# Splitting a third of the second MLP's weights during the first MLP, with the float64 clamp on GpSimd and buffer pools of its own for each MLP

## The chip, the cores and the metric

One core of one Trainium2 chip runs the whole program. The metric is the device time of one execution in microseconds (us), as the median of several executions. Engines are called by the profile's names: PE is TensorE (matmul), PEld its weight load, DVE VectorE, ACT ScalarE, POOL GpSimd, SP SyncE, which here only issues DMAs.

## What is computed

The reference chains three parts (float64 in, float32 out), cut here to what matters:

```python
# attention with 32 learned memory slots; 4 batches, 8 heads, 576 positions, head size 64
a = softmax(phi, axis=positions);  k_m = a.T @ k;  v_m = a.T @ v
x = softmax(q @ k_m.T / 8) @ v_m            # -> 2304 tokens x 512
h = x @ w_in;  x = (h * sigmoid(1.702 * h)) @ w_out          # MLP A: 512 -> 2048 -> 512
xn = x / sqrt(mean(x * x) + 1e-6) * rms_g
g = xn @ w_gate;  val = xn @ w_val
out = (g * sigmoid(g) * val) @ w_out2                        # MLP B: 512 -> 1536 -> 512
```

## The kernel before, in words

Matmuls run in float32r, three products for one (high x high, low x high, high x low), so every operand exists as a high part `h` (a cast) and a low part `l` (`sub_lo`: the full value minus `h`).

The weights arrive as float64 bit patterns. One half of 128 x 512 values is loaded as a `raw` tile by SP (`w_load`, L137 to L149) and turned into float32 by `to_f32`: the absolute value of the upper word on ACT (L162), then on DVE a clamp (L163), a shift (L167) and two ops that put sign and lower bits together (L171, L174). `w_conv` (MLP A) casts to `h` (`copy`, L113 on POOL or L117 on ACT), subtracts for `l` on POOL (L120) and stores both to a cache in DRAM. `b_split` does the same for MLP B.

The 2304 tokens are worked in two passes (`pr` 0 and 1) of two batches each. MLP A goes through 8 groups of 256 hidden columns in each pass, each group in 4 steps of 288 tokens: `vm_part` folds the attention's values into the weights (L499), `a_g1` makes the hidden values (L531, then `gf` and `gr` by ACT, L537 and L539, and POOL, L120), `a_g2` multiplies by `w_out` (L560) and adds to `x2` on DVE (L568). In pass 0 a group's four weight halves are converted one group ahead, in pass 1 they come back from the cache (`w_again`, L199). The attention of the first two batches runs ahead of MLP A, that of the other two beside its pass 0.

MLP B takes 12 chunks of 128 hidden columns in each pass, with a Strassen-like scheme of seven products: weight tiles 0 to 3 are the gate half, two tiles of sums of gate and value halves (`b_sums`, L231, four DVE ops of 128 x 256) and half a value tile, tile 4 is `w_out2`. One chunk is prepared by `b_prep`: three loads, three `to_f32`, the sums, five `b_split`, each with a store to the cache. `b_unit` makes one chunk for one half of the pass's tokens: seven products on PE (L681), their evacuation on ACT and DVE (L693 to L707), `ph` (L711) and `pl` (L120 on POOL in pass 0, on DVE in pass 1). `b_out` multiplies two chunks by `w_out2` (L733) and adds on DVE (L742). In pass 0 chunk c+1 is prepared beside the units of chunk c; chunk 0 is prepared beside the last group of MLP A. In pass 1 all chunks come back from the cache (`b_again`, L252).

Between the MLPs stand `norm_1` to `norm_4` (squares on ACT, sums on POOL, L585 and L587, scaling on DVE, L627) and `x_sums` and `x_split` (sums and split of the normalised tokens, L647, L658, L120). For pass 0 they run beside MLP A's pass 1, for pass 1 beside MLP B's pass 0, two steps after each unit from chunk 2 on, and `x_sums`/`x_split` of pass 1 with the last chunk.

Each engine and each DMA queue runs its instructions in one fixed order. That order is made at build time by the tile framework's scheduler, from the order in which the program states its steps (the list of steps, `run`, and the loop at the end) and from when a tile of a pool is free. The pools: `raw` 2 tiles, `cv` 5 (work tiles of a conversion), `w` 10 (weight tiles of both MLPs, and work tiles), `gp` 5 (`gr` in MLP A, `ph` in MLP B), `tmp` 4 (`gf` in MLP A, `sg` and `pf` in MLP B).

## Time and profile before

| what | value |
|---|---|
| time, median of 3 runs (lowest to highest) | 948.96 us (948.2 to 949.48) |
| the profiled execution: time, span | 947.55 us, 945.8 us |
| granted TensorE clock, mean | 0.971 of full speed |
| busy share of the span: PE, PEld | 91%, 84% |
| busy share of the span: DVE, ACT, POOL | 71%, 50%, 38% |
| HBM read, written | 97.26 MB, 49.81 MB |

How to read it: the profiled execution lies 1.41 us under the median and 1.75 us over its own span. A busy PE is not a PE at its peak, as matmuls are pipelined, so the shares say less of PE than the distance in time between equal pieces of work. DVE, ACT and POOL stand still for a good part of the span as a whole; what a change is worth depends on the stage it touches. Stretches of time are given as 75:250, in us from the span's start.

### The profile page before, as it was taken

To read this page: it belongs to the slowest core of one execution; us is meant where nothing else is said; L and a number is where in the kernel's file an instruction comes from. 1 tells how busy PE (TensorE), PEld (TensorE's weight loads), DVE (VectorE), ACT (ScalarE), POOL (GpSimd) and SP (SyncE) were. 2 spreads that over 40 slices of the span, in tenths; PEclk is the share of its full clock that TensorE was granted. 3 is DMA by queue.
4 is the path that set the end of the run, shared out by engine and by line. 5 is a ranking of instruction groups with operands and counts; after the bars stand their busy time and mean duration, and the time that the engine had idled before them with its cause. 6 is when DMAs were issued, how large, how long until landed. Compare 5 with 4: busy or idle time off the path is not lost.

```text
span 945.8 us, 16130 instructions
## 1 busy us (share of the span) xinstructions
...
## 2 busy tenths in 40 slices
...
GB/s 213 250 221 90 178 169 230 206 202 210 140 156 90 90 90 89 126 144 114 125 164 189 192 176 171 164 167 134 245 245 89 212 135 122 145 146 132 146 57 100
DMA packets 63966, 148.11 MB, mean 157 GB/s; under 512 B 5776, under 2 KB 30352, under 8 KB 63888
## 3 DMA queue, kind: packets, MB, share of 16 engines
...
HBM read 97.26 MB, written 49.81 MB: 155 GB/s over the span
## 4 chain that ended last, share of the span: by engine, by line
PE 55%; DVE 22%; DMA 8%; ACT 7%; issue 5%; POOL 1%; SPq 1%; ACTq 0%; DVEq 0%; POOLq 0%
PE pg L560 14%; PE pg L733 11%; PE px L681 10%; PE pg L531 8%; PE pw L681 5%; DMA raw_a_in<-in_moe_w_in_dram 4%; PE py L681 3%; DVE cv L171 2%; DVE t L647 2%; DVE cv L174 2%; DVE x L120 2%; DVE s L231 2%; DVE x L568 2%; PE pvm L499 2%; DVE cv L163 2%
## 5 line engine op out<-in xcount | busy, mean ns | idle before, releaser
L560 PE MATMUL pg<-gr,a_outh 128*128 128x288 f32 x1024 | 239.4, 304 | 14.5 <-DVE x L568 9.8
L560 PEld LDWEIGHTS pg<-gr,a_outh 128*128 128x128 f32 x1024 | 177.2, 192 | 20.2 <-DVE x L568 14.2
L681 PE MATMUL px<-x,b_w 128*128 128x256 f32 (+1 forms) x1152 | 182.2, 298 | 12.2 <-ACT sg L693 3.0
L681 PEld LDWEIGHTS px<-x,b_w 128*128 128x128 f32 x1152 | 165.4, 190 | 21.7 <-DVE sg L703 4.2
L120 POOL TENSOR_TENSOR gr<-gf,gr 128x288 fp32r<-128x288 f32 x128 | 111.4, 885 | 128.9 <-ACT gr L539 125.6
L560 PE MATMUL pg<-gr,a_outl 128*128 128x288 f32 x512 | 153.1, 299 | 0.0
L568 DVE TENSOR_TENSOR x<-x,pg 128x288 f32<-128x288 f32 x224 | 98.5, 447 | 52.9 <-PE pg L560 52.1
L733 PE MATMUL pg<-b_w,ph 128*128 128x512 f32 x432 | 132.6, 398 | 2.9 <-DVE oacc L742 2.5
L681 PE MATMUL pw<-x,b_w 128*128 128x320 f32 (+1 forms) x576 | 97.8, 297 | 5.1 <-ACT pf L695 2.7
L560 PEld LDWEIGHTS pg<-gr,a_outl 128*128 128x128 f32 x512 | 98.4, 192 | 0.0
L681 PEld LDWEIGHTS pw<-x,b_w 128*128 128x128 f32 x576 | 84.7, 189 | 8.7 <-ACT pf L695 3.5
L733 PEld LDWEIGHTS pg<-b_w,ph 128*128 128x128 f32 x432 | 78.1, 190 | 16.2 <-DVE oacc L742 3.8
L733 PE MATMUL pg<-b_w,pl 128*128 128x512 f32 x216 | 80.7, 395 | 0.0
L742 DVE TENSOR_TENSOR oacc<-oacc,pg 128x512 f32<-128x512 f32 x90 | 59.4, 680 | 24.5 <-PE pg L733 24.5
L537 ACT ACTIVATE gf<-pg 128x288 f32<-128x288 f32 x128 | 51.7, 411 | 38.6 <-POOL gr L120 18.1
L120 POOL TENSOR_TENSOR b_w<-cv,b_w 128x512 fp32r<-128x512 f32 (+1 forms) x36 | 45.0, 1252 | 62.3 <-ACT b_w L117 56.1
L539 ACT CAST gr<-gf 128x288 fp32r<-128x288 f32 x128 | 52.3, 432 | 28.7 <-PE pg L560 26.7
L163 DVE TENSOR_SCALAR cv<-cv 128x512 f32<-128x512 f32 x68 | 41.4, 613 | 32.2 <-ACT cv L162 32.1
L681 PE MATMUL py<-x,b_w 128*128 128x256 f32 (+1 forms) x288 | 49.4, 300 | 7.0 <-DVE pf L707 5.2
L697 ACT COPY sg<-px 128x256 f32<-128x256 f32 (+1 forms) x48 | 19.1, 398 | 70.9 <-PE px L681 67.8
L711 ACT CAST ph<-pf 128x512 fp32r<-128x512 f32 (+1 forms) x48 | 32.2, 671 | 41.9 <-DVE pf L707 41.7
L681 PEld LDWEIGHTS py<-x,b_w 128*128 128x128 f32 x288 | 42.0, 190 | 10.7 <-DVE pf L707 8.0
...
## 6 DMA issues: line engine op xcount, KB each, us to landing
...
```

The lines of the kernel that those rows point to most:

```text
L120: eng.tensor_tensor(out=lo, in0=full, in1=hi.bitcast(F32), op=ALU.subtract)
L163: nc.vector.tensor_scalar(out=t.bitcast(F32), in0=t.bitcast(F32), scalar1=MINW, scalar2=MAXW, op0=ALU.max, op1=ALU.min,)
L531: nc.tensor.matmul(ps[:, :HALF], lhsT=a[:, b, c, f], rhs=at[:, y, c, n], start=(i == 0), stop=(i == 5),)
L537: nc.scalar.activation(out=gf[:, :HALF], in_=ps[:, :HALF], func=AF.Gelu_apprx_sigmoid)
L539: nc.scalar.copy(out=gr[:, 0], in_=gf[:, :HALF])
L560: nc.tensor.matmul(ps[:, :HALF], lhsT=wo[a][:, fc, es], rhs=gr[fc][:, y], start=(i == 0), stop=(i == 5),)
L568: nc.vector.tensor_tensor(out=acc[:, e, n], in0=acc[:, e, n], in1=ps[:, :HALF], op=ALU.add)
L681: nc.tensor.matmul(ps, lhsT=w[j][:, o : o + P], rhs=xk[k][:, y, xb], start=(first and i == 0), stop=(i == 5), skip_group_check=not (first ...
L697: nc.scalar.copy(out=sg[:, 1], in_=px)
L711: nc.scalar.copy(out=ph, in_=flat)
L733: nc.tensor.matmul(ps, lhsT=lhs, rhs=w[fc][:, y * 512 : y * 512 + 512], start=(i == 0), stop=(i == 5),)
L742: nc.vector.tensor_tensor(out=o, in0=o, in1=ps, op=ALU.add)
```

## The change

- `to_f32` gets an engine for the clamp, POOL by default. In MLP A's pass 0 all clamps but one (`w2[0]`, still DVE) go to POOL; so do those of `gate` and `val` of all MLP B chunks, and that of `o2` for chunks 0 to 3.
- Chunks 0 to 3 of MLP B (`NPRE = 4`) are prepared beside MLP A's pass 1 (`second_side`, three steps after each unit, interleaved with norm and split of pass 0). Their four sums go to POOL too. Their split tiles are only stored to the cache; MLP B's pass 0 reads them back with `b_again`, and prepares chunks 4 to 11 as before.
- The norm of pass 1 runs five steps after each unit from chunk 0 on.
- Pools: MLP A has `rawa` with 3 tiles, `gf` with 3 and `gr` with 5 of the size needed; they are released together with the attention's pools after MLP A, and MLP B's `rawb` 2, `tmp` 4, and `gp` with 5 `ph` and 5 `pl` are laid into that memory. `norm_1` of pass 1 takes its two squares from `tmp` instead of `w`.

```diff
+    NPRE = 4
-    rawp = ctx.enter_context(tc.tile_pool(name="raw", bufs=2))
-    gpp = ctx.enter_context(tc.tile_pool(name="gp", bufs=5))
-    tmp = ctx.enter_context(tc.tile_pool(name="tmp", bufs=4))
+    rawa = tc.alloc_tile_pool(name="rawa", bufs=3, side="right")
+    gfp = tc.alloc_tile_pool(name="gf", bufs=3, side="right")
+    grp = tc.alloc_tile_pool(name="gr", bufs=5, side="right")
...
-    def to_f32(hf):
+    def to_f32(hf, clamp=G):
...
-        nc.vector.tensor_scalar(
+        clamp.tensor_scalar(
             out=t.bitcast(F32), in0=t.bitcast(F32), scalar1=MINW, scalar2=MAXW,
...
-        y = wt.setdefault(("b", c), {})[j] = wtile(f"b_w{j}_{c}")[:, : 2 * n]
+        y = wtile(f"b_w{j}_{c}")[:, : 2 * n]
+        if c >= NPRE:
+            wt.setdefault(("b", c), {})[j] = y
...
-        b_split(c, 4, to_f32(("b", c, "o2")), A, G)
+        b_split(c, 4, to_f32(("b", c, "o2"), G if c < NPRE else V), A, G)
...
-            nc.vector.tensor_tensor(out=out, in0=a, in1=b, op=op)
+            (G if c < NPRE else V).tensor_tensor(out=out, in0=a, in1=b, op=op)
...
-        sq = [wtile(f"sq{i}_{pr}_{t}", F32)[:, : 2 * N] for i in range(2)]
+        sq = [
+            (wtile(f"sq{i}_{pr}_{t}", F32) if pr == 0 else tmp.tile([P, TW], F32, tag="val", name="sq"))
+            [:, : 2 * N] for i in range(2)
+        ]
...
+    def second_side():
+        loads = iter([("b", c, w) for c in range(NPRE) for w in ("gate", "val", "o2")])
+        others = iter([
+            norm_side(0, 0), x_side(0, 0, 0), [*x_side(0, 0, 1), *norm_side(0, 1)],
+            x_side(0, 1, 0),
+        ])
+        for _ in range(2):
+            yield w_load, next(loads)
+        for c in range(NPRE):
+            for s in b_steps(c):
+                yield s
+                hf = next(loads, None) if s[0] in (b_gate, b_val, b_o2) else None
+                if hf:
+                    yield w_load, hf
+            yield from next(others)
...
             if key == ("a", 1, 0) and t == 1:
-                side, per = first_norm(), 2
-            if key == ("a", 1, 7):
-                side, per = prep, 3
+                side, per = second_side(), 3
+            if key == ("a", 1, 7) and t == 1:
+                b_again(0)
...
+    for pool in (grp, gfp, rawa, kmp, vlp):
+        pool.release()
+    two = dict(side="right", reuse_waits="tile")
+    raws[0] = rawb = tc.alloc_tile_pool(name="rawb", bufs=2, **two)
+    tmp = tc.alloc_tile_pool(name="tmp", bufs=4, **two)
+    gpp = tc.alloc_tile_pool(name="gp", bufs=5, **two)
...
-            else:
-                prep = b_prep(c + 1) if pr == 0 else iter([(b_again, c + 1)])
+            elif pr or c + 1 < NPRE:
+                prep = iter([(b_again, c + 1)])
+            else:
+                prep = b_prep(c + 1)
...
-                for s in islice(norms, 2 if c >= 2 else 0):
+                for s in islice(norms, 5):
```

The code moves by up to 23 lines: L163 becomes L165, L113 L115, L120 L122, L231 L235, L252 L258, L199 L201.

**Place 1: POOL in MLP A's pass 0, around the weights of group 6.** `a_6_in` and `a_6_out` are the group's weight tiles, `cv` the work tile of a conversion. Before:

```order
L113 TENSOR_SCALAR a_6_inh<-cv 128x512
L120 TENSOR_TENSOR a_6_inl<-cv,a_6_inh 128x512
L120 TENSOR_TENSOR gr<-gf,gr 128x288 x2
L113 TENSOR_SCALAR a_6_inh<-cv 128x512
L120 TENSOR_TENSOR a_6_inl<-cv,a_6_inh 128x512
L113 TENSOR_SCALAR a_6_outh<-cv 128x512
L120 TENSOR_TENSOR a_6_outl<-cv,a_6_outh 128x512
L113 TENSOR_SCALAR a_6_outh<-cv 128x512
L120 TENSOR_TENSOR gr<-gf,gr 128x288 x2
L120 TENSOR_TENSOR a_6_outl<-cv,a_6_outh 128x512
```

With the change:

```order
L115 TENSOR_SCALAR a_6_inh<-cv 128x512 x2
L122 TENSOR_TENSOR gr<-gf,gr 128x288
L165 TENSOR_SCALAR cv<-cv 128x512 x2
L122 TENSOR_TENSOR gr<-gf,gr 128x288
L122 TENSOR_TENSOR a_6_inl<-cv,a_6_inh 128x512
L115 TENSOR_SCALAR a_6_outh<-cv 128x512
L122 TENSOR_TENSOR a_6_inl<-cv,a_6_inh 128x512
L122 TENSOR_TENSOR gr<-gf,gr 128x288 x2
L327 TENSOR_TENSOR kmisc_0_2166<-kmisc_0_2166 96x768
L115 TENSOR_SCALAR a_6_outh<-cv 128x512
L122 TENSOR_TENSOR gr<-gf,gr 128x288
L165 TENSOR_SCALAR cv<-cv 128x512 x2
```

The clamps (L165) now stand between the splits of `gr` that PE waits for and the splits of the weights; they come in pairs, ahead of the group's own casts.

**Place 2: POOL in MLP A's pass 1, after the norm of the second token tile.** `x_0_0` are split tokens for MLP B, `b_w_1` and `s` its chunk 1. Before:

```order
L120 TENSOR_TENSOR gr<-gf,gr 128x288 x4
L120 TENSOR_TENSOR x_0_0_4145<-x_0_821,x_0_0_4145 128x256
L120 TENSOR_TENSOR gr<-gf,gr 128x288 x2
L120 TENSOR_TENSOR x_0_0_4362<-x_0_821,x_0_0_4362 128x256
L120 TENSOR_TENSOR x_0_0_4145<-t_4140,x_0_0_4145 128x2x256
L120 TENSOR_TENSOR x_0_0_4362<-t_4357,x_0_0_4362 128x2x256
L120 TENSOR_TENSOR gr<-gf,gr 128x288 x14
```

With the change:

```order
L122 TENSOR_TENSOR b_w_1_4415<-cv,b_w_1_4415 128x512
L122 TENSOR_TENSOR gr<-gf,gr 128x288
L235 TENSOR_TENSOR s_4409<-cv 128x256
L235 TENSOR_TENSOR s_4410<-cv 128x256
L235 TENSOR_TENSOR s_4409<-s_4409,cv 128x256
L165 TENSOR_SCALAR cv<-cv 128x512
L235 TENSOR_TENSOR s_4410<-cv,s_4409 128x256
L122 TENSOR_TENSOR gr<-gf,gr 128x288
L122 TENSOR_TENSOR b_w_1_4479<-s_4409,b_w_1_4479 128x512
L122 TENSOR_TENSOR gr<-gf,gr 128x288
L122 TENSOR_TENSOR b_w_1_4483<-s_4410,b_w_1_4483 128x512
L122 TENSOR_TENSOR gr<-gf,gr 128x288 x2
```

Where fourteen splits of `gr` followed each other, one or two now stand between ops of a chunk: five ops in a row at the longest place shown.

**Place 3: SP's DMA queue from MLP A's last weights on.** `a_7` are group 7's weights from the cache, `raw_b` loads for a conversion, `b_w_0` and `b_w_1` tiles of chunks 0 and 1. Before:

```order
L199 DMA a_7_outh<-cache 128x1024
L199 DMA a_7_outl<-cache 128x1024
L139 DMA raw_b_val<-in_moe_w_val_dram 128x4x256
L137 DMA raw_b_o_5930<-in_moe_w_out_dram 128x1024
L139 DMA raw_b_gate<-in_moe_w_gate_dram 128x4x256
L139 DMA raw_b_val<-in_moe_w_val_dram 128x4x256
L137 DMA raw_b_o_6100<-in_moe_w_out_dram 128x1024
```

With the change:

```order
L201 DMA a_7_outh<-cache 128x1024
L201 DMA a_7_outl<-cache 128x1024
L141 DMA raw_b_gate<-in_moe_w_gate_dram 128x4x256
L141 DMA raw_b_val<-in_moe_w_val_dram 128x4x256
L258 DMA b_w_0_5765<-cache_103 128x1024
L258 DMA b_w_0_5767<-cache_103 128x1024
L258 DMA b_w_0_5769<-cache_103 128x1024
L258 DMA b_w_0_5771<-cache_103 128x512
L258 DMA b_w_0_5773<-cache_103 128x1024
L258 DMA b_w_1_6083<-cache_103 128x1024
```

After the last weights of MLP A the queue now holds two loads for chunk 4 and then 20 reloads, of chunks 0 to 3, before the next load for a conversion.

## Rows read from the trace of the kernel before

**Rows 1.** Busy time of each engine by stretch, in us, with instruction counts.

```profile
core 0: us, PE busy (x) PEld busy (x) DVE busy (x) ACT busy (x) POOL busy (x), PEclk, DMA share, GB/s
...
75.00:250.00 175.00, 153.19 (x1164) 144.75 (x1165) 146.50 (x281) 103.53 (x233) 99.47 (x104) 0.91 0.58 186
...
300.00:450.00 150.00, 147.94 (x1132) 146.58 (x1131) 95.62 (x203) 94.47 (x222) 70.06 (x77) 1.00 0.31 111
...
500.00:700.00 200.00, 182.65 (x1135) 164.21 (x1136) 172.34 (x300) 108.27 (x208) 104.19 (x78) 1.00 0.52 184
700.00:750.00 50.00, 41.76 (x239) 36.92 (x238) 38.83 (x60) 20.94 (x46) 16.87 (x12) 0.93 0.50 161
750.00:900.00 150.00, 150.00 (x966) 140.49 (x965) 69.50 (x135) 46.26 (x96) 0.00 (x0) 1.00 0.40 137
```

**Rows 2.** First product of MLP A, by group: ns min/median/max, first and last start.

```profile
L531 PE MATMUL pg<-attnT,vm_0h x64: 288/295/588, 60.1 to 318.5; 128*128 128x288 f32 x64
L531 PE MATMUL pg<-attnT,vm_1h x64: 290/294/399, 103.5 to 339.2; 128*128 128x288 f32 x64
...
L531 PE MATMUL pg<-attnT,vm_7h x64: 290/295/302, 268.7 to 460.2; 128*128 128x288 f32 x64
```

**Rows 3.** The SiLU of MLP B's units, line L705, in 480:728 and in 728:946.

```profile
L705 ACT ACTIVATE sg<-sg x24: 615/684/743, 484.2 to 711.5; 128x512 f32<-128x512 f32 x12, 128x640 f32<-128x640 f32 x12
...
L705 ACT ACTIVATE sg<-sg x24: 627/698/742, 730.4 to 927.5; 128x512 f32<-128x512 f32 x12, 128x640 f32<-128x640 f32 x12
```

**Rows 4.** Waits in 75:250: who for whom, us in total, times, longest.

```profile
ACT cv L162 <- DMA raw_a_out<-in_moe_w_out_dram: 16.8, 8, 4.2
...
ACT cv L162 <- DMA raw_a_in<-in_moe_w_in_dram: 12.1, 7, 2.8
...
PE pg L531 <- ACT gf L537: 6.9, 4, 3.7
```

**Rows 5.** Waits of the whole span, SP's DMA queue.

```profile
SPq L147 <- DVE cv L174: 93.9, 15, 12.0
SPq L149 <- DVE cv L174: 70.7, 14, 8.5
```

**Rows 6.** Groups of instructions, whole span: busy us, mean ns of one, idle before.

```profile
L163 DVE TENSOR_SCALAR cv<-cv 128x512 f32<-128x512 f32 x68 | 41.4, 613 | 32.2 <-ACT cv L162 32.1
L167 DVE TENSOR_SCALAR cv<-cv 128x512 uint32<-128x512 uint32 x68 | 39.3, 581 | 0.5
...
L627 DVE SCALAR_TENSOR_TENSOR x<-x,rg,rb 128x256 f32<-128x256 f32 (+1 forms) x32 | 20.1, 686 | 4.6 <-ACT rb L622 4.4
...
L231 DVE TENSOR_TENSOR s<-cv 128x256 f32<-128x256 f32 x24 | 16.9, 735 | 0.0
...
L585 POOL TENSOR_TENSOR sq<-sq,sq 128x512 f32<-128x512 f32 (+1 forms) x8 | 11.9, 1487 | 2.3 <-ACT sq L581 2.3
...
L171 DVE SCALAR_TENSOR_TENSOR cv<-raw_b_val,cv 128x512 uint32<-128x512 uint32 x12 | 11.0, 914 | 0.1
...
L174 DVE SCALAR_TENSOR_TENSOR cv<-raw_b_val,cv 128x512 uint32<-128x512 uint32 x12 | 9.4, 787 | 0.1
```

**Rows 7.** Groups of instructions on POOL, shapes kept apart, whole span.

```profile
L120 POOL TENSOR_TENSOR gr<-gf,gr 128x288 fp32r<-128x288 f32 x128 | 111.4, 885 | 128.9 <-ACT gr L539 125.6 <-PE pg L560 2.0 <-DVE vll L120 0.9
...
L120 POOL TENSOR_TENSOR b_w<-cv,b_w 128x512 fp32r<-128x512 f32 x24 | 33.5, 1396 | 53.5 <-ACT b_w L117 47.2 <-issue 6.1 <-POOL pl L120 0.2
...
L120 POOL TENSOR_TENSOR b_w<-cv,b_w 128x256 fp32r<-128x256 f32 x12 | 11.6, 966 | 8.9 <-ACT b_w L117 8.9
...
L113 POOL TENSOR_SCALAR a_outh<-cv 128x512 fp32r<-128x512 f32 x14 | 9.7, 696 | 24.7 <-DVE cv L174 18.8 <-DVE rv L367 5.9
```

**Rows 8.** DVE's clamp and its add from PSUM in 75:250: ns min/median/max, starts.

```profile
L163 DVE TENSOR_SCALAR cv<-cv x26: 395/427/2074, 76.3 to 244.9; 128x512 f32<-128x512 f32 x26
...
L568 DVE TENSOR_TENSOR x<-x,pg x69: 426/442/456, 119.9 to 248.7; 128x288 f32<-128x288 f32 x69
```

**Rows 9.** Timeline around 486 us: start, duration, engine, line, idle before.

```profile
485.08 0.41 DVE L231 TENSOR_TENSOR s<-s,cv 128x256 f32<-128x256 f32 x1
...
485.84 1.29 POOL L120 TENSOR_TENSOR b_w<-cv,b_w 128x512 fp32r<-128x512 f32 x1 [3.56 <-ACT b_w L117]
...
486.12 1.30 DVE L231 TENSOR_TENSOR s<-cv,s 128x256 f32<-128x256 f32 x1
```

More of the change, by code (lines that the diff above doesn't have):

```diff
@@ L101, in wtile, with ttile @@
         return wp.tile([P, 1024], dt, tag="w", name=name)
-    def ttile(pool, name, dt=F32):
-        tag = {id(cvp): "cv", id(gpp): "gp", id(tmp): "val"}[id(pool)]
-        return pool.tile([P, TW], dt, tag=tag, name=name)
+    def ttile(name, dt=F32):
+        return cvp.tile([P, TW], dt, tag="cv", name=name)
     def psum(pool, name):
@@ L131, in w_load @@
     def w_load(hf):
-        raw = loaded[hf] = rawp.tile([P, 1024], U32, tag="raw", name="raw_" + "_".join(map(str, hf)))
+        raw = loaded[hf] = raws[0].tile([P, 1024], U32, tag="raw", name="raw_" + "_".join(map(str, hf)))
         if hf[0] == "b":
@@ L177, in to_f32, with w_conv @@
         return t.bitcast(F32)
-    def w_conv(hf, to_h=G, to_l=G):
+    def w_conv(hf, clamp=G, to_h=G, to_l=G):
         key = hf[:-1]
-        x = to_f32(hf)
+        x = to_f32(hf, clamp)
         if hf[-1] == 0:
@@ L246, in b_prep @@
         yield b_o2, c
+    def b_prep(c):
+        for w in ("gate", "val", "o2"):
+            yield w_load, ("b", c, w)
+        yield from b_steps(c)
     def b_again(c):
@@ L336, in att_k3s @@
         o = o.rearrange("p (h c m) -> p h c m", h=4, c=1)
-        y = ttile(tmp, "y")[:CP, :384]
+        y = gfp.tile([P, 384], F32, tag="val", name="y")[:CP]
         y = y.rearrange("p (h c m) -> p h c m", h=4, c=3)
@@ L535, in a_g1 @@
                     i += 1
-            gf = ttile(tmp, "gf")
+            gf = gfp.tile([P, 384], F32, tag="val", name="gf")
             nc.scalar.activation(out=gf[:, :HALF], in_=ps[:, :HALF], func=AF.Gelu_apprx_sigmoid)
-            gr = ttile(gpp, "gr", F32R).rearrange("p (x n) -> p x n", x=2)[:, :, :HALF]
+            gr = grp.tile([P, 2, HALF], F32R, tag="gr", name="gr")
             nc.scalar.copy(out=gr[:, 0], in_=gf[:, :HALF])
@@ L640, in x_sums @@
         t12, t34 = (
[L641 removed]
+            ttile(y).rearrange("p (i n) -> p i n", i=2)[:, :, :N] for y in ("t12", "t34")
         )
@@ L688, in b_unit @@
         px, pw, py = (psum(*x)[:, :N] for x in ((ps_mm, "px"), (ps_att, "pw"), (ps_mm, "py")))
-        sg = ttile(tmp, "sg")[:, : 2 * N].rearrange("p (t n) -> p t n", t=2)
-        pf = ttile(tmp, "pf")[:, : 2 * N].rearrange("p (t n) -> p t n", t=2)
+        sg = tmp.tile([P, TW], F32, tag="val", name="sg")[:, : 2 * N].rearrange("p (t n) -> p t n", t=2)
+        pf = tmp.tile([P, TW], F32, tag="val", name="pf")[:, : 2 * N].rearrange("p (t n) -> p t n", t=2)
         add = dict(op=ALU.add)
```

49 lines of the change are left out of this document (18 added, 31 removed).

## The prediction, made before the changed kernel was run

> **What bounds the kernel now.** I read the table of stretches first. In the second passes of both MLPs PE is busy all but fully: 1.4% idle in 300:450, none to speak of in 750:900 [rows 1]. In the first passes, where weights are converted, it idles 12% in 75:250 and 8.7% in 500:700, and DVE stands at 84 and 86%, against 64 and 46% in the second passes. Then the pace of equal work. Group 1's to group 7's first products of MLP A start 268.7 - 103.5 = 165.2 us apart in pass 0, 27.5 us a group; in pass 1 group 0 to 7 take 460.2 - 318.5 = 141.7 us, 20.2 a group [rows 2]. Part of the 7.3 us between them is attention on PE beside pass 0. In MLP B 23 steps of the SiLU take 227.3 us in pass 0 and 197.1 in pass 1: 19.8 and 17.1 us a chunk [rows 3]. So conversion costs up to 6 x 7.3 = 44 us in MLP A and 12 x 2.7 = 32 in MLP B; the change works on these and pays in MLP A's pass 1.
>
> Which link of a conversion is late stands in the waits: ACT waits 28.9 us for raw loads in 75:250, in order, with `gf` behind, and PE waits 6.9 us for `gf` [rows 4]. The loads are late because SP waits for DVE's last op of an earlier conversion to free one of two raw tiles, 165 us over the span [rows 5]. DVE is the head of that ring.
>
> **Term 1, MLP A's pass 0.** 26 of the span's 68 clamps lie in 75:250 [rows 8]. At 613 ns [rows 6] they take 15.9 us off DVE, 9 points of its 84%. POOL's nearest op to a clamp is its cast of the same shape, 696 ns [rows 7]: 18.1 us, POOL goes from 57 to 67%. Between the passes 20 points of DVE go with 7.3 us a group, so 9 points are worth at most 3.3 us, some 20 over six groups; attention in that slope makes this a bound. From the other side: a conversion now goes ACT, POOL, DVE instead of ACT, DVE, POOL's clamps stand ahead of `gr` splits that PE needs, and each clamp is slower there; that can eat all of it, or more (rival 3). The clamps' wait for ACT adds little for what is queued behind them on POOL: `gr` needs a `gf` that stands on ACT behind the same absolute values. The third raw tile can give at most the 6.9 us of that wait [rows 4] and is inside the 20. I take **-5**, a quarter: PE itself waited only 6.9 us for `gf`, so much of the slope is no wait for DVE.
>
> **Term 2, MLP A's pass 1.** Here chunks 1 to 3 are new (chunk 0 was prepared in the last group before). On DVE a chunk is three times a shift and two combining ops, 3 x (0.581 + 0.914 + 0.787) = 6.85 us [rows 6], three of them 20.6 us in 8 x 20.2 = 162 us: DVE goes from 64 to 76%. On POOL a chunk is three clamps, four sums of 128 x 256, four splits of 128 x 512 and one of 128 x 256: 3 x 0.696 + 4 x 0.966 + 4 x 1.396 + 0.966 = 12.5 us [rows 7], the sums priced as the split of that shape; three chunks are 37.5 us, POOL goes from 47 to 70%. PE idles 1.4% at 64% of DVE and 8.7% at 86% [rows 1]; a line between them gives 5.4% at 76%: 4.0 points of 162 us, **+6.5**. Bounds: 0, if PE's work covers it all as it does now, and 7.3 points, +11.8, if the pass falls to the idle share of 500:700. The ten `w` tiles, of which chunk tiles now hold some while group weights come back, are inside that upper end. DMA: three chunks bring 1.6 MB of loads and 2.4 MB of stores each, 12 MB in 162 us or 73 GB/s on top of 111; 75:250 moves 186 [rows 1], so 0.
>
> **Term 3, MLP B's pass 0, chunks 0 to 3.** They come back from the cache as in pass 1, so 4 x 2.7 = -10.8 us at best. Against it: the norm of pass 1 is packed into them, and its squares take two of the four `tmp` tiles while POOL adds them twice, so a unit's `sg` or `pf` may wait; four pairs of sums at 1.487 us [rows 6] are at most 6 us, half is taken: **-8**. The low bound of the gain is -4.8. On SP the reloads stand behind two raw loads that need the memory of released pools; chunk 0's are issued during MLP A's last group, and if they are late the first unit of MLP B is, by a few us (700:750, the other hand-over, idles 8.2 us altogether [rows 1]). I take 0 here, since what the two loads wait for are MLP A's own last ops, which run ahead of that unit.
>
> **Term 4, chunks 4 to 11.** DVE loses two clamps a chunk (1.23 us) and the norm's scaling, 16 of the 32 ops at 0.686 us [rows 6] that lay over ten chunks, 1.1 us each: 2.3 of the 172.34 x 19.8 / 200 = 17.1 us that DVE works per chunk. POOL takes the clamps (1.4 us) and loses its share of the norm. At best the chunk runs at pass 1's pace, 8 x 2.7 = 21.6 us; at worst nothing. DVE would stand at 75%, about half way between 86 and 64; with the lower half of that, 1 us a chunk, **-8**.
>
> The x sums with the last chunk (700:750) stay. Sum: -5 + 6.5 - 8 - 8 = -14.5; 947.55 - 14.5 = 933.05 for an execution like the profiled one, and with the 1.41 us to the median **934.5 us**. 0.2% (1.9 us) is about what a measurement of this kernel can tell from no change. Half of what terms 1, 3 and 4 give (10.5 us) lost or gained once more puts this case at 924 to 945.
>
> **Rival 1: DVE's relief is paid in full.** For it: it heads the ring of raw tiles [rows 5], and the two stretches with much idle PE are those with a loaded DVE [rows 1]. Against: attention shares in the difference of the passes. Term 1 at its bound -20, pass 1 at 0, chunks 0 to 3 -10.8, the rest -8: -38.8, 910 us. Chance 0.20.
>
> **Rival 2: MLP A's pass 1 gives it back.** POOL's `gr` split follows ACT at once there, and PE's second product follows `gr`; with up to five chunk ops between two splits (some 5 us in a step of 5 us) PE waits. Term 1 is 0, pass 1 +11.8, chunks 0 to 3 -8, 4 to 11 -6: -2, 947 us. Chance 0.13.
>
> **Rival 3, slower: DVE and POOL hold each other up.** At 486 us a sum that takes DVE 0.41 us took 1.30: it began inside a split on POOL and ended 0.3 us after it [rows 9]. The clamp's median is 427 ns and its longest 2074, while the add from PSUM beside it never exceeds 456 [rows 8]. So DVE's 613 ns are partly waiting for POOL, and a clamp that holds DVE 427 ns by itself would, on POOL, hold it 696: the shared time grows by 0.27 us each. Then the 26 clamps cost 7.0 instead of giving 5, pass 1, where DVE meets 37.5 us more of POOL, goes to its bound of +11.8, and in MLP B 16 clamps cost 4.3 of the 8 that chunks 0 to 3 gain, with nothing for the others: 7.0 + 11.8 - 3.7 = +15.1, 964 us. It decides once DVE's two-operand ops in pass 0 slow by more than the clamps free: 26 x 0.427 = 11.1 us over the 26 conversions' three other DVE ops, 0.14 us each. Against it: term 3 is there whatever the engines share, and pass 1 has idle time on both. Chance 0.17.
> The Trainium skill ("SBUF — State Buffer", section "Who interferes with whom") says why: the two engines share one pair of SBUF ports under an exclusive lock, and a DVE op with two SBUF inputs, or one in a two-port mode, excludes a GpSimd op that reads SBUF. By that rule, moving DVE's SBUF work to POOL frees no shared time at all, terms 1 and 4 vanish, and the time is that of this rival; the clamp's 2074 ns and the sum's 1.30 us agree on the lock [rows 8, 9], and no row of this kernel shows a clamp on POOL.
>
> **How the numbers follow.** The forecast keeps 0.50. Rival 1 is faster, rival 3 slower; of rival 2's 0.13 I put 0.03 on faster, 0.08 on within 0.2% and 0.02 on slower. Faster 0.73, same 0.08, slower 0.19. The range 908 to 955 takes in the forecast, rival 2, most of rival 1 and the near side of rival 3; some 0.1 is left out above and 0.08 below.
>
> **What would show it.** Term 1: groups of pass 0 at 26.5 to 27 us, ACT's wait for raw loads well under 28.9 us, and DVE near 76% in 75:250; the same 27.5 or more with longer combining ops is rival 3. Term 2: pass 1 at about 21 us a group with 5% of PE idle; 20.2 is rival 1, over 21.5 rival 2 or 3, and then PE's waits name `gr`. Term 3: SiLU steps of chunks 0 to 3 at 17 to 18 us a chunk, with no gap of PE at the first unit of MLP B. Term 4: 18.5 to 19 us a chunk from chunk 4 on. The prediction is wrong if MLP B's pass 0 gains under 8 us, or if pass 1 of MLP A costs over 12.

## The result and the profile after the change

| | before | with the change |
|---|---|---|
| median of 20 runs (lowest to highest) | 948.24 us (944.2 to 952.51) | 952.24 us (948.1 to 960.35) |
| ratio to before, 95% interval | | 1.0051 (1.0028 to 1.0074) |
| the profiled execution: time, span | 947.55 us, 945.8 us | 948.33 us, 946.5 us |

Slower by 0.5%. The forecast was 934.5 us, faster. The profiled execution of the changed kernel lies 3.9 us under its median, so the trace shows one of its better executions.

The clamp first. Its groups by line, engine and shape in the changed kernel (duration in ns min/median/max, first and last start), beside the shift that follows it on DVE:

```profile
L165 POOL TENSOR_SCALAR cv<-cv x59: 1906/1917/2464, 31.1 to 676.2; 128x512 f32<-128x512 f32 x59
...
L165 DVE TENSOR_SCALAR cv<-cv x9: 411/413/1805, 76.5 to 684.7; 128x512 f32<-128x512 f32 x9
...
L169 DVE TENSOR_SCALAR cv<-cv x68: 357/655/1860, 33.0 to 687.7; 128x512 uint32<-128x512 uint32 x68
```

A clamp takes POOL 1.92 us, not the 0.70 of the cast in [rows 7]. Its shortest is 1906 ns, so this is its own length and no waiting. The same stretches as in [rows 1]:

```profile
75.00:250.00 175.00, 153.69 (x1228) 146.68 (x1225) 147.81 (x267) 109.72 (x240) 159.97 (x134) 0.95 0.60 199
300.00:450.00 150.00, 143.92 (x1066) 141.20 (x1065) 100.95 (x191) 99.26 (x227) 110.80 (x106) 0.99 0.47 164
500.00:700.00 200.00, 179.98 (x1078) 161.43 (x1079) 165.83 (x263) 93.12 (x182) 121.10 (x81) 0.97 0.48 168
700.00:750.00 50.00, 44.96 (x269) 40.62 (x268) 34.21 (x55) 19.53 (x44) 15.20 (x11) 0.93 0.48 150
750.00:900.00 150.00, 149.71 (x960) 139.81 (x960) 68.99 (x132) 46.57 (x97) 0.00 (x0) 1.00 0.41 142
```

In 75:250 POOL goes from 57 to 91%. DVE, with one clamp left in this window, is as busy as before (147.81 against 146.50 us), but the window now holds 1228 matmuls instead of 1164. For the same columns of matmul (69:232 of the changed kernel, counted as below) DVE is busy 138.4 us: some 8 us less, half of what the clamps took there (15.6 us). PE is busy as long as before (153.69 against 153.19 us), so it idles as long as before; it gets through more because its granted clock is 0.95 of full speed instead of 0.91. In 300:450 PE now idles 4.1% where it idled 1.4%.

Nevertheless MLP A's pass 0 became faster. First products by group, as [rows 2]:

```profile
L537 PE MATMUL pg<-attnT,vm_0h x64: 290/295/606, 59.0 to 304.8; 128*128 128x288 f32 x64
L537 PE MATMUL pg<-attnT,vm_1h x64: 289/295/398, 99.0 to 324.8; 128*128 128x288 f32 x64
...
L537 PE MATMUL pg<-attnT,vm_7h x64: 289/295/443, 256.1 to 464.4; 128*128 128x288 f32 x64
```

Group 7 starts at 256.1 us instead of 268.7, 12.6 earlier. By the end of pass 1 (464.4 against 460.2) nothing of that is left.

To place gains over the whole span I add up the columns that PE's matmuls stream, in order of their start. Both programs issue 6,008 matmuls with the same sum, so the time at which a kernel reaches the sum that the kernel before had at 300 us tells its lead there. This is good to some 2 us, since pieces of work changed places. Changes of the lead by stretch, in us of the kernel before (+ is gained), each from one profiled execution:

| stretch of before | work | changed kernel | forecast |
|---|---|---|---|
| 0:300 | attention, MLP A pass 0 | +14.6 | +5 |
| 300:475 | MLP A pass 1 | -11.1 | -6.5 |
| 475:560 | MLP B, about chunks 0 to 3 | -1.9 | +8 |
| 560:725 | MLP B, about chunks 4 to 11 | -1.4 | +8 |
| 725:940 | MLP B pass 1 | -0.4 | 0 |

Not all of this is waiting. Over the columns of 75:250 the lead grows by 12.0 us, but PE's idle time falls only from 21.8 to 20.3 us. What falls is the time in which PE is busy at half clock, 1.2 instead of 2.4 GHz: 29.5 us before, 12.4 us now. At 1026 columns per busy us at half clock and 1982 at full clock (kernel before, this stretch) that is worth some 8 us, by my estimate. Over the whole span the mean clock is 0.971 in both profiled executions; the changed kernel has its half clock later (0.97 in 500:700, where it was 1.00). Why it moved is not shown.

How pass 1 loses time shows best near its end. The timeline of the changed kernel around 450 us (start, duration, engine, line, idle before and who ended it; L656 are the sums of `x_sums`, L574 the adds from PSUM):

```profile
449.80 0.81 DVE L574 TENSOR_TENSOR x<-x,pg 128x288 f32<-128x288 f32 x2
450.51 2.78 POOL L122 TENSOR_TENSOR b_w<-s,b_w 128x512 fp32r<-128x512 f32 x2
450.53 1.62 DVE L656 TENSOR_TENSOR t<-x 128x320 f32<-128x320 f32 x1
...
452.44 1.21 DVE L656 TENSOR_TENSOR t<-x,t 128x320 f32<-128x320 f32 x1
453.26 2.46 POOL L122 TENSOR_TENSOR b_w<-cv,b_w 128x256 fp32r<-128x256 f32 x2
...
458.70 1.47 DVE L656 TENSOR_TENSOR t<-x 128x320 f32<-128x320 f32 x1
459.78 2.04 POOL L122 TENSOR_TENSOR gr<-gf,gr 128x288 fp32r<-128x288 f32 x2
460.09 1.07 DVE L656 TENSOR_TENSOR t<-x,t 128x320 f32<-128x320 f32 x1
461.09 0.81 DVE L574 TENSOR_TENSOR x<-x,pg 128x288 f32<-128x288 f32 x2
...
461.58 0.61 PE L566 MATMUL pg<-gr,a_outh 128*128 128x288 f32 x1 [1.70 <-DVE x L574]
461.82 0.48 DVE L656 TENSOR_TENSOR t<-x,t 128x320 f32<-128x320 f32 x1
```

POOL works without a gap, on chunk 3's splits (`b_w`) among others. The sums on DVE shown beside it take 1.07 to 1.62 us; the one at 461.82, with POOL idle from 461.82 on, takes 0.48. DVE's add from PSUM stands in order behind them, and PE waits 1.70 us for it. DVE and POOL hold each other up, as in rival 3, but at another op than the clamp. Right before the 1.70 us POOL's ops are splits of `x` and `gr`, which the kernel before has too; that the chunk's ops bring them together with the sums is likely, not shown.

### The profile page after: what moved, and what is told of

Its sections match the earlier page's. It is cut to its first block, busy times and chain, and to the rows that moved or that the text cites. A ratio compares the mean times of both kernels' runs of the same rounds, so it can differ in the third digit from the quotient of the medians.

```text
span 946.5 us, 16159 instructions
## 1 busy us (share of the span) xinstructions
PE 856.7 (91%) x6008; PEld 799.9 (85%) x6008; DVE 660.4 (70%) x1199; ACT 471.6 (50%) x1015; POOL 499.5 (53%) x428
## 3 DMA queue, kind: packets, MB, share of 16 engines
q10 hardware_dynamic: 13248, 45.09, 12.6%
## 4 chain that ended last, share of the span: by engine, by line
PE 51%; DVE 20%; POOL 9%; issue 7%; DMA 6%; ACT 5%; SPq 2%; ACTq 0%; POOLq 0%; DVEq 0%
PE pg L566 12%; PE pg L741 11%; PE px L690 10%; PE pg L537 6%; PE pw L690 5%; POOL cv L165 3%; PE py L690 3%; DVE cv L173 2%; DMA raw_b_val<-in_moe_w_val_dram 2%; DVE cv L176 2%; DVE t L656 2%; DVE cv L169 2%; DMA raw_a_out<-in_moe_w_out_dram 2%; DVE x L574 2%; DVE x L122 1%
## 5 line engine op out<-in xcount | busy, mean ns | idle before, releaser
L566 PEld LDWEIGHTS pg<-gr,a_outh 128*128 128x128 f32 x1024 | 175.0, 191 | 22.6 <-DVE x L574 17.5
L574 DVE TENSOR_TENSOR x<-x,pg 128x288 f32<-128x288 f32 x224 | 96.3, 447 | 64.4 <-PE pg L566 63.1
L165 POOL TENSOR_SCALAR cv<-cv 128x512 f32<-128x512 f32 x59 | 119.8, 2035 | 39.8 <-ACT cv L164 37.2
L122 POOL TENSOR_TENSOR gr<-gf,gr 128x288 fp32r<-128x288 f32 x128 | 115.0, 910 | 45.8 <-ACT gr L545 42.1
L169 DVE TENSOR_SCALAR cv<-cv 128x512 uint32<-128x512 uint32 x68 | 56.2, 826 | 17.9 <-POOL cv L165 17.7
L122 POOL TENSOR_TENSOR pl<-pf,ph 128x512 fp32r<-128x512 f32 (+1 forms) x24 | 36.9, 1537 | 34.7 <-ACT ph L719 34.7
L122 POOL TENSOR_TENSOR b_w<-cv,b_w 128x512 fp32r<-128x512 f32 (+1 forms) x36 | 45.6, 1268 | 14.6 <-ACT b_w L119 14.3
L690 PE MATMUL py<-x,b_w 128*128 128x256 f32 (+1 forms) x288 | 51.7, 309 | 1.6 <-DVE pf L716 0.8
```

What stands on the lines that cost most here:

```text
L122: eng.tensor_tensor(out=lo, in0=full, in1=hi.bitcast(F32), op=ALU.subtract)
L165: clamp.tensor_scalar(out=t.bitcast(F32), in0=t.bitcast(F32), scalar1=MINW, scalar2=MAXW, op0=ALU.max, op1=ALU.min,)
L169: nc.vector.tensor_scalar(out=t, in0=t, scalar1=3, scalar2=0x3FFFFFFF, op0=ALU.logical_shift_left, op1=ALU.bitwise_and,)
L566: nc.tensor.matmul(ps[:, :HALF], lhsT=wo[a][:, fc, es], rhs=gr[fc][:, y], start=(i == 0), stop=(i == 5),)
L574: nc.vector.tensor_tensor(out=acc[:, e, n], in0=acc[:, e, n], in1=ps[:, :HALF], op=ALU.add)
L690: nc.tensor.matmul(ps, lhsT=w[j][:, o : o + P], rhs=xk[k][:, y, xb], start=(first and i == 0), stop=(i == 5), skip_group_check=not (first ...
```

## Experiments

All lines and diffs are against the changed kernel. Each was timed in five rounds against the kernel before on the same chip, except `e8_forms`. The groups ran on different chips, so across groups the ratios compare better than the medians. Ratios are to the kernel before, with the 95% interval; the gains by stretch of all that were profiled follow each group, read as above.

### First group: the clamps and the early split

**e1_clamp_dve**, all clamps on DVE:

```diff
-        clamp.tensor_scalar(
+        nc.vector.tensor_scalar(
```

> All clamps back on DVE, everything else as changed. Theory 1 (the clamp on POOL is the loss: it took 1.92 us there where 0.70 was priced, and DVE's two-operand ops wait while it runs): MLP A's pass 1 costs about 5 us instead of the 11 it cost, chunks 4 to 11 of MLP B gain what was forecast, 8 us; 930 to 940 us. Theory 2 (the early split of chunks 0 to 3 is the loss, and the clamps on POOL made the 15 us that MLP A's pass 0 gained): pass 0 falls back to a lead of 5 us or less over the kernel before, the rest stays; 955 to 965 us.

Measured: 962.0 us, 1.0131 (1.0104 to 1.0159). Slower, as theory 2 had it.

**e2_no_pre**, no chunk split early (the norm and split of pass 0 alone beside MLP A's pass 1):

```diff
-    NPRE = 4
+    NPRE = 0
...
-        for _ in range(2):
-            yield w_load, next(loads)
+        for x in others:
+            yield from x
...
-            if key == ("a", 1, 7) and t == 1:
-                b_again(0)
+            if key == ("a", 1, 7) and t == 0:
+                side = b_prep(0)
```

> No chunk split early (chunk 0 beside the last group of MLP A, chunks 1 to 11 in MLP B, as before the change), clamps on POOL as changed, pools as changed. Theory 1 (POOL clamp): pass 1 of MLP A loses nothing, so its 15 us of lead stay to its end, but all twelve chunks of MLP B's pass 0 then carry POOL clamps, at 0.3 us of loss for each of chunks 4 to 11 so far and more where the norm lies beside: 938 to 948 us. Theory 2 (early split): the 11 us of pass 1 come back whole and MLP B stays level with the kernel before: 935 to 939 us.

Measured: 960.89 us, 1.0134 (1.0105 to 1.0163). Worse than both theories allowed: the early split is worth 8.7 us to the rest of the change by the medians, 8 us by the ratios.

**e3_no_pre_clamp_dve**, both edits together.

> Neither early split nor clamps on POOL: what is left of the change are the pools (three raw tiles in MLP A, own gf and gr tiles, own ph and pl) and the earlier norm of pass 1. Theory 1: the third raw tile makes most of the 15 us of pass 0, so 935 to 942 us. Theory 2: the clamps on POOL made them, so within 3 us of the kernel before, 945 to 951 us.

Measured: 963.09 us, 1.0157 (1.0128 to 1.0186). Both theories missed: what is left, which looked harmless (pools, the norm of pass 0 at three steps a unit and that of pass 1 at five), costs 13 to 15 us.

**e4_clamp_b_dve**, MLP B's clamps on DVE, MLP A's on POOL:

```diff
-        clamp.tensor_scalar(
+        (V if hf[0] == "b" else clamp).tensor_scalar(
```

> Clamps of MLP A on POOL as changed, all clamps of MLP B on DVE, chunks 0 to 3 split early as changed. Theory 1: pass 1 of MLP A loses about 5 us instead of 11, MLP B's pass 0 gains 8 to 16; pass 0 of MLP A as changed; 930 to 940 us, and with all clamps on DVE it is about the same or faster. Theory 2: only pass 0's 15 us are kept and the early split costs as it did: 948 to 954 us.

Measured: 947.5 us, 0.9977 (0.995 to 1.0004). Between the two expectations: 4.7 us under the changed kernel's median, in theory 1's direction for MLP B, but pass 1 lost as much as with the clamps on POOL.

| gain by stretch, us | 0:300 | 300:475 | 475:560 | 560:725 |
|---|---|---|---|---|
| e1_clamp_dve | -1.3 | -14.4 | -1.8 | +4.3 |
| e2_no_pre | +13.5 | -7.0 | -14.6 | -6.4 |
| e3_no_pre_clamp_dve | +7.2 | -5.4 | -9.7 | -4.8 |
| e4_clamp_b_dve | +5.4 | -11.5 | -0.4 | +4.0 |

Two readings. In 560:725 the POOL clamps cost 5 us (-1.4 against +4.0): over the same columns PE idles 19.9 instead of 17.2 us, and is busy at half clock 11.2 instead of 6.0 us. The stretch 565:725 of the changed kernel and then of e4_clamp_b_dve, with columns as in [rows 1], and DVE's groups in it (busy us, mean ns), shows why:

```profile
565.00:725.00 160.00, 141.45 (x829) 125.69 (x828) 142.63 (x224) 67.49 (x138) 97.00 (x65) 0.96 0.52 182
```

```profile
565.00:725.00 160.00, 142.81 (x846) 126.01 (x845) 142.06 (x243) 68.59 (x139) 75.19 (x53) 0.98 0.53 184
```

Changed kernel:

```profile
L169 DVE TENSOR_SCALAR cv<-cv 128x512 uint32<-128x512 uint32 x19 | 20.0, 1052 | 5.7 <-POOL cv L165 5.6
L173 DVE SCALAR_TENSOR_TENSOR cv<-raw_b_val,cv 128x512 uint32<-128x512 uint32 x6 | 9.4, 1569 | 0.2
...
L165 DVE TENSOR_SCALAR cv<-cv 128x512 f32<-128x512 f32 x7 | 4.9, 706 | 0.0
```

e4_clamp_b_dve:

```profile
L169 DVE TENSOR_SCALAR cv<-cv 128x512 uint32<-128x512 uint32 x20 | 13.9, 697 | 0.1
L165 DVE TENSOR_SCALAR cv<-cv 128x512 f32<-128x512 f32 x20 | 13.7, 686 | 2.8 <-ACT cv L164 2.8
L173 DVE SCALAR_TENSOR_TENSOR cv<-raw_b_val,cv 128x512 uint32<-128x512 uint32 x7 | 8.8, 1252 | 0.1
```

Thirteen clamps fewer (8.8 us) leave DVE as busy as with them, 142.63 against 142.06 us. The shift's mean grew from 697 to 1052 ns, and DVE waited 5.6 us for POOL's clamps besides. What holds the shift is not the clamp on POOL but the split that follows it there. The first shift of this kind in the stretch, in the changed kernel (start, duration):

```profile
570.35 1.91 POOL L165 TENSOR_SCALAR cv<-cv 128x512 f32<-128x512 f32 x1
571.55 0.49 DVE L715 TENSOR_TENSOR pf<-pf,sg 128x320 f32<-128x320 f32 x1 [0.79 <-ACT sg L714]
572.23 1.29 POOL L122 TENSOR_TENSOR pl<-pf,ph 128x512 fp32r<-128x512 f32 x1
572.29 1.52 DVE L169 TENSOR_SCALAR cv<-cv 128x512 uint32<-128x512 uint32 x1 [0.25 <-POOL cv L165]
```

Beside the clamp a two-input op on DVE takes 0.49 us, its usual time. When the clamp ends, POOL takes up its next split at once, DVE the shift 0.06 us later, and the shift ends 0.29 us after the split. Of the 19 shifts in the stretch 12 are held to the end of a split like this, 8 of them by a split that POOL had taken up, right behind its clamp, less than 0.1 us before; in e4_clamp_b_dve 6 of 20 are held. Over the whole changed kernel 20 shifts begin inside a 128x512 split, with a median of 1497 ns, and 11 inside a clamp on POOL, with a median of 420 ns, all over before the clamp is. So the clamp frees DVE while it runs, and the order behind it takes the time back.

The Trainium skill ("SBUF — State Buffer", section "Who interferes with whom") says that a DVE op with two SBUF inputs contends with a GpSimd op that reads SBUF, and that whoever issues first blocks the other for the whole instruction. The splits agree. The clamps on POOL do not: 25 of DVE's two-input combining ops (L173, L176) begin inside one, with a median of 693 ns, where 676 is their usual time.

And in 475:560 the kernels without early chunks lose 10 to 15 us, those with them next to nothing: reloading chunks 0 to 3 is worth 8 to 13 us, as term 3 had it at best. Something else takes it back.

### Second group: the norm's pace, the raw tiles, the clamp's price

**e5_norm_pace**, the norm of pass 1 as before the change:

```diff
-                for s in islice(norms, 5):
+                for s in islice(norms, 2 if c >= 2 else 0):
```

> The changed kernel with the norm of pass 1 back at the old pace (two steps a unit from chunk 2 on, not five from chunk 0 on). Theory N (chunks 0 to 3 lost their forecast 8 to 11 us because the norm's ACT, POOL and DVE work was packed into them): chunks 0 to 3 gain about 8 us against the changed kernel, part of it is lost again in chunks 4 to 11, 943 to 948 us. Rival R (the reloads are the loss there, late behind stores and raw loads): the same 950 to 954 us.

Measured: 960.97 us, 1.0103 (1.006 to 1.0146). Theory N had the direction for chunks 0 to 3 (4.7 of its 8 us) and was wrong for the whole: beside the POOL clamps of chunks 4 on, the norm costs more than it did beside the reloads.

**e6_norm_pace_b_dve**, the same edit in e4_clamp_b_dve.

> The same with MLP B's clamps on DVE too (MLP A's on POOL). If the norm's packing and the POOL clamps of MLP B cost independently: the 5 us that MLP B's clamps on DVE gave and the gain of the norm's pace add up, 938 to 943 us. If the early split has little to give whatever stands beside it: 945 to 950 us.

Measured: 946.97 us, 0.9973 (0.9949 to 0.9997). The gains do not add up: the second expectation.

**e7_raw2**, two raw tiles in MLP A:

```diff
-    rawa = tc.alloc_tile_pool(name="rawa", bufs=3, side="right")
+    rawa = tc.alloc_tile_pool(name="rawa", bufs=2, side="right")
```

> The changed kernel with two raw tiles in MLP A instead of three. If the third raw tile makes a good part of pass 0's lead: ACT's waits for raw loads return to some 29 us in 75:250 and the time rises by 5 us or more, 957 to 962 us. If the clamps on POOL alone make it: 950 to 955 us.

Measured: 965.13 us, 1.0158 (1.012 to 1.0197), 13 us over the changed kernel by the medians, 10 by the ratios, more than expected. ACT waits 25.1 us for raw loads in 75:250, near the expected 29, against 10.4 in the changed kernel.

| gain by stretch, us | 0:300 | 300:475 | 475:560 | 560:725 |
|---|---|---|---|---|
| e5_norm_pace | +3.2 | -11.3 | +2.8 | -11.1 |
| e6_norm_pace_b_dve | +9.4 | -10.9 | +4.9 | -1.9 |
| e7_raw2 | -5.9 | -12.5 | -1.9 | -1.6 |

At the old pace the norm gives back 4.7 and 5.3 us in chunks 0 to 3 and costs 9.7 and 5.9 in the later ones. The first stretch shows the spread of single executions: the changed kernel and e5 run the same order there and stand at +14.6 and +3.2. The profiled execution of e7_raw2 (971.29 us) lies 6.2 us over its median, so its -5.9 is low too.

**e8_forms**, one execution: POOL's clamp in four forms by turns. Behind the last two forms stands a clamp on DVE.

```diff
+            G.tensor_scalar(out=f, in0=f, scalar1=MINW, scalar2=None, op0=ALU.max)
+            G.tensor_scalar(out=f, in0=f, scalar1=MAXW, scalar2=None, op0=ALU.min)
...
+            G.tensor_scalar(out=f, in0=f, scalar1=MINW, scalar2=0.0, op0=ALU.max, op1=ALU.add)
...
+            G.tensor_scalar(out=f, in0=f, scalar1=1.0, scalar2=0.0, op0=ALU.mult, op1=ALU.add)
```

> Prices of forms of the clamp on POOL, taken in turn: as changed (maximum, minimum with two constants), two ops with one constant each, maximum then an add of 0, multiply by 1 then add 0 (the form of the cast) in place; DVE clamps again behind the last two. If the two bounds in one op make the 1.92 us: one-constant ops at about 0.7 us. If maximum or minimum as such is slow on POOL: each one-constant op over 1 us and the multiply-and-add at 0.7. If it is the fp32 output in place that is slow: all about 1.9 us. The time itself tells nothing, as ops are added.

The groups by line: L171 maximum, L172 minimum, L174 maximum and add, L177 multiply and add:

```profile
L171 POOL TENSOR_SCALAR cv<-cv x15: 1489/1497/2485, 32.2 to 683.1; 128x512 f32<-128x512 f32 x15
...
L172 POOL TENSOR_SCALAR cv<-cv x15: 1490/1494/1737, 36.7 to 686.3; 128x512 f32<-128x512 f32 x15
...
L174 POOL TENSOR_SCALAR cv<-cv x15: 1922/1930/2378, 34.7 to 698.5; 128x512 f32<-128x512 f32 x15
...
L177 POOL TENSOR_SCALAR cv<-cv x15: 614/624/1062, 42.0 to 704.9; 128x512 f32<-128x512 f32 x15
```

A maximum or a minimum alone takes 1.49 us on POOL, with a second op 1.92; multiply and add, same shape and in place, 0.62. It is the operation that is dear, more than the second constant (0.43 us) and not the output. The cast of [rows 7] was the wrong neighbour to price the clamp by.

### Third group: what of the change is worth keeping

**e9_a_only**: the edits of e2_no_pre, e4_clamp_b_dve and e5_norm_pace together, and the norm of pass 0 at its old pace:

```diff
-                side, per = second_side(), 3
+                side, per = second_side(), 2
```

> Only MLP A's part of the change and the pools: no chunk split early, MLP B's clamps on DVE, norms of both passes at the old pace (two steps a unit), three raw tiles and MLP A's clamps on POOL. If the 5 to 7 us that pass 1 of MLP A lost without any early chunk (in the two kernels without them) come from the norm's quicker pace: pass 1 loses 0 to 2 us, pass 0 leads by about 9, MLP B is level: 939 to 943 us. If they come from the pools (three gf tiles for four): pass 1 loses 5 us or more again: 945 to 949 us.

Measured: 939.92 us, 0.9904 (0.9871 to 0.9937). Faster than both kernels, and inside the first expectation, but not by its sum: the profile has pass 0 at +16.1 instead of about 9, and MLP B's pass 0 at -6.8 instead of level. Pass 1 loses 3.1 us: the quicker norm made a part of what the kernels without early chunks lost there (5.4 and 7.0), not all.

**e10_sums_dve**, e6 with the sums of the early chunks on DVE:

```diff
-            (G if c < NPRE else V).tensor_tensor(out=out, in0=a, in1=b, op=op)
+            V.tensor_tensor(out=out, in0=a, in1=b, op=op)
```

> Early split of four chunks with MLP B's clamps and sums on DVE and the norm at its old pace (only the sums differ from the run norm_pace_b_dve). If POOL's load makes the 11 us that pass 1 loses (POOL gives up 16 sums of 0.74 to 1.18 us, 13 us, for 6.6 us of DVE): pass 1 loses 6 to 9 us, 942 to 945 us. If DVE's order is what PE waits for (its adds from PSUM stand behind the conversion): 11 us or more again, 947 to 951 us.

Measured: 945.9 us, 0.9966 (0.9942 to 0.999), between the two expectations, and no difference to e6 that the intervals could tell. The sums' engine does not make pass 1's loss.

**e11_gf4**, e6 with four `gf` tiles (`bufs=3` to `bufs=4` in pool `gf`).

> The run norm_pace_b_dve with four gf tiles instead of three. If the pools cost pass 1 its time (ACT's gf waits for POOL's gr split to free a tile): pass 1 loses 5 to 7 us instead of 11, 940 to 944 us. If not: within 2 us of that run, 945 to 949 us.

Measured: 944.07 us, 0.9945 (0.9923 to 0.9966). Inconclusive: 2.9 us under e6, with overlapping intervals, and pass 1 lost 9.3 us where 10.9 were lost.

**e12_npre2**, e6 with two early chunks:

```diff
-    NPRE = 4
+    NPRE = 2
...
-            yield from next(others)
+            for _ in range(2):
+                yield from next(others)
```

> The run norm_pace_b_dve with two early chunks instead of four. If the loss of pass 1 goes with the chunks: it loses 8 to 9 us instead of 11, chunks 2 and 3 of MLP B give back 3 us, so no change within 2 us, 945 to 949 us. If an early chunk is worth more in MLP B than it costs in MLP A (head start for the conversions): slower, 950 us or more.

Measured: 943.07 us, 0.9942 (0.9907 to 0.9976). Faster than either expectation: pass 1 loses only 2.9 us where 8 to 9 were expected, and MLP B's pass 0 loses 2.6.

| gain by stretch, us | 0:300 | 300:475 | 475:560 | 560:725 |
|---|---|---|---|---|
| e9_a_only | +16.1 | -3.1 | -3.3 | -3.5 |
| e10_sums_dve | +9.9 | -10.8 | +4.7 | -0.5 |
| e11_gf4 | +6.3 | -9.3 | +4.5 | -0.7 |
| e12_npre2 | +8.7 | -2.9 | +1.0 | -3.6 |

With four early chunks pass 1 loses 9 to 14 us in every kernel, with two as little as with none, 3 to 7, whether the chunks' clamps and sums run on POOL or DVE. In MLP B's pass 0 they give 10 to 11 us against e9 (475:725: e6 +3.0, e10 +4.2, e9 -6.8). So the early split moves the price of a conversion from one MLP to the other. Its 8.7 us in the first group are what it avoids, the packed norm and POOL clamps beside the conversions of chunks 0 to 3: without early chunks 475:560 loses 14.6 us with both (e2), 9.7 with the norm alone (e3) and 3.3 with neither (e9). With neither, the kernel without it is 7 us faster (e9 against e6).

### Fourth group: third raw tile or clamps on POOL

**e13_raw3_only**, e9 with all clamps on DVE.

> The run a_only with all clamps on DVE: three raw tiles and the pools alone. If the third raw tile makes pass 0's lead: 938 to 943 us, as with the clamps on POOL. If the clamps on POOL make half of it or more: 945 to 952 us.

Measured: 952.51 us, 1.0031 (1.0005 to 1.0058), nearest to the second expectation.

**e14_clamp_only**, e9 with two raw tiles.

> The run a_only with two raw tiles: clamps of MLP A on POOL alone. A clamp of 1.92 us lengthens each conversion, and with two raw tiles the next load waits for it: if the clamp pays only where a third raw tile hides its length, 950 to 957 us, slower than the kernel before; if it pays by itself, 940 to 946 us.

Measured: 955.85 us, 1.0087 (1.0054 to 1.012), the first expectation.

Neither makes up alone for what the pools cost from 300 us on (9 to 11 us in each of these kernels): both are slower than the kernel before, and together they are the 939.92 us of e9. The waits of 75:250 tell why. e14_clamp_only:

```profile
ACT cv L164 <- DMA raw_a_out<-in_moe_w_out_dram: 14.8, 9, 3.9
...
ACT cv L164 <- DMA raw_a_in<-in_moe_w_in_dram: 12.1, 6, 4.1
```

e13_raw3_only:

```profile
PE pg L566 <- DVE x L574: 9.0, 8, 2.0
...
PE pvm L505 <- ACT gf L543: 6.1, 4, 1.9
...
ACT cv L164 <- DMA raw_a_out<-in_moe_w_out_dram: 4.5, 4, 2.1
...
ACT cv L164 <- DMA raw_a_in<-in_moe_w_in_dram: 2.1, 1, 2.1
```

e9_a_only, with both:

```profile
ACT cv L164 <- DMA raw_a_out<-in_moe_w_out_dram: 7.7, 4, 2.8
...
ACT cv L164 <- DMA raw_a_in<-in_moe_w_in_dram: 5.3, 4, 4.4
PE pg L566 <- DVE x L574: 4.6, 6, 1.8
```

With two tiles ACT still waits 26.9 us for loads, as it did before (28.9); a conversion of 1.5 us more keeps its raw tile longer. With three tiles and the clamps on DVE that wait is 6.6 us, but PE waits 9.0 us for DVE's adds, which stand behind the conversions. With both, 13.0 and 4.6. The stretch itself, columns as in [rows 1], in the order e14, e13, e9:

```profile
75.00:250.00 175.00, 148.20 (x1164) 141.06 (x1164) 129.35 (x239) 96.66 (x216) 135.18 (x117) 0.92 0.53 166
75.00:250.00 175.00, 147.16 (x1212) 140.25 (x1211) 148.72 (x291) 108.41 (x235) 106.09 (x108) 0.97 0.61 196
75.00:250.00 175.00, 153.61 (x1236) 146.85 (x1235) 146.05 (x268) 107.83 (x240) 157.94 (x135) 0.96 0.62 196
```

PE idles 26.8 and 27.8 us with one of the two parts, 21.4 with both, and 21.8 in the kernel before. Either part alone adds idle time, both together add none; what e9 gains on the kernel before in this stretch is pace, at a clock of 0.96 against 0.91.

**e15_half**, e9 with only the first half of each of MLP A's weights clamped on POOL:

```diff
+        (clamp if hf[0] == "a" and hf[-1] == 0 else V).tensor_scalar(
```

> The run a_only with only the first half of each MLP A weight clamped on POOL, the second on DVE (POOL some 77% busy in pass 0 instead of 90%, DVE 3 points more). If POOL's load gives part of the gain back: 934 to 938 us. If DVE's relief is what pays: 942 to 947 us, half way to the run raw3_only.

Measured: 959.22 us, 1.0096 (1.007 to 1.0121). Outside both expectations, and slower than all clamps on either engine. The loss arises early: by the columns its profile is 12 us behind the kernel before at 110 us, where e9 is 6 ahead, and regains 6 by 300. The cause stays open.

**e16_sq_w**, e9 with the norm's squares of pass 1 in `w` tiles:

```diff
-            (wtile(f"sq{i}_{pr}_{t}", F32) if pr == 0 else tmp.tile([P, TW], F32, tag="val", name="sq"))
+            wtile(f"sq{i}_{pr}_{t}", F32)
```

> The run a_only with the norm's squares of pass 1 in w tiles, as before the change. If the squares in tmp tiles hold up the units of MLP B: 7 us of its pass 0 come back, 933 to 937 us. If not: within 2 us of that run, 938 to 943 us.

Measured: 937.05 us, 0.9859 (0.9828 to 0.989), the fastest. Its interval overlaps e9's, but its profile shows the gain where it was expected, in 475:725.

| gain by stretch, us | 0:300 | 300:475 | 475:560 | 560:725 |
|---|---|---|---|---|
| e13_raw3_only | +9.9 | -2.6 | -3.3 | -3.4 |
| e14_clamp_only | -4.2 | -5.6 | -3.4 | -1.5 |
| e15_half | -5.9 | -2.6 | -2.2 | -3.6 |
| e16_sq_w | +15.4 | -3.0 | -1.8 | +2.0 |

The profiles of e13_raw3_only (946.85 us, 5.7 under its median) and of e14_clamp_only (961.52 us, 5.7 over it) mislead in 0:300. In the later stretches like kernels agree within about 1 us (300:475 of the changed kernel, e4, e5 and e6: 10.9 to 11.5 lost), so most of the spread lies in the first. Taking the later stretches' losses off the difference of the medians puts 0:300 at about +5 for the third tile alone, +2 for the clamps alone and +18 for both. The same working gives +11 for the changed kernel and +7 for e5 with one order, so it is good to some 4 us. By the medians the clamps on POOL are worth 952.51 - 939.92 = 12.6 us beside the third tile.

## Why the prediction was wrong

**What bounds the kernel** held in part: conversions make both first passes slow, and the raw tiles' ring and DVE are its two links in MLP A. But I read DVE's 84% as work that could be carried away. It is partly waiting for POOL's splits: of 15.6 us of clamps some 8 are gained for the same work. And PE's idle time in 75:250 hardly fell.

**Term 1**, -5 forecast. The profile gained 14.6. The ten kernels with MLP A's clamps on POOL and three raw tiles, the changed one among them, gained 10 on average, 3.2 to 16.1. The direction was right, but partly by luck: of the 12.0 us that the profile gained in 75:250 some 8 are a higher granted clock, which the prediction did not reckon with, and PE's idle time gave 1.5. The working was wrong in two places: the clamp's 0.696 us were 1.92, and the third tile, held to be worth at most 6.9 us of PE's wait, decides whether the rest pays: without it the stretch gains about 2 us by the medians (the two profiles, both of long executions, lose 4 to 6).

**Term 2**, +6.5 forecast, 11.1 lost; its upper bound of 11.8 held. About 3 us of this are there with no early chunk and the old norm pace (e9, e13, e15, e16; 5.6 in e14), 2 to 4 more with the quicker norm (e2, e3), and the rest comes with the chunks, not in proportion to them: with two, e12 lost 2.9. DVE rose to 67%, not 76%: PE's idle did not follow DVE's load, as the line between two stretches supposed. Waits of single ops for the other engine, as at 450 us, are what the trace shows; clamps or sums on DVE did not change the loss, and which ops of an early chunk cost most was not taken further apart.

**Term 3**, -8 forecast, 1.9 lost. The reload's gain was right (8 to 13 us measured, 10.8 forecast). What failed is the price of what lies against it: the packed norm was put at 3 us and costs about 5 (e5, e6), and the new pools with the squares in `tmp`, hardly priced, cost about 3 more (e9, e13).

**Term 4**, -8 forecast, 1.4 lost. This step failed outright: "DVE loses two clamps a chunk" was counted as 1.23 us of DVE time saved. In the runs DVE stays as busy (142.63 us with 13 clamps fewer, 142.06 with them), because the shift behind a clamp on POOL starts together with POOL's next split and is held to its end. With the same clamps on DVE the stretch gains 4.0 us instead of losing 1.4; beside the norm it loses 1.9 instead of 11.1. The clamps on POOL thus cost 5 to 9 us here, about half of it as idle time of PE and half at half clock. With terms 3 and 4 MLP B's pass 0 lost 3.3 us where 16 were to be gained; a gain under 8 was named beforehand as a sign of being wrong. The other half of the term held: moving the norm away is worth 5.9 us (e4 against e6).

**Rival 3** named the two engines rightly and the holder wrongly: by it the clamp itself, once on POOL, holds DVE. The splits do (12 of 19 shifts in 565:725), and no shift that began inside a clamp on POOL was held to its end. That work moved to POOL frees no shared time, as the prediction drew from the port rule, is not borne out by the same rows. The rival's 7 us of loss in MLP A's pass 0 did not come; the runs with and without the third raw tile show that ACT's and SP's ring mattered there. The time came out nearest to rival 2's 947 us, by another way: its first term was 0 and MLP B was to gain 14, and here the first term paid for all others. The range held the time, but the forecast sign was wrong.
